# A planner's priorities get a table of offsets, and its durations are set anew

## The chip, the cores and the metric

One core of one Trainium2 chip runs the kernel as one program. The metric is the device time of one execution in microseconds. Every time of an engine below comes from one profiled execution.

## The reference, cut to what matters

```python
# attention-like part: x is (2, 3008, 256)
X = np.fft.fft(x, axis=1)            # over the 3008 positions
X = np.fft.fft(X, axis=2)            # over the 256 features
x = X.real                            # 6016 tokens x 256
# first MLP: w_in 256x2048, w_out 2048x256
h = x @ w_in
g = np.maximum(h, 0.0) ** 2
x = g @ w_out
# second MLP, same sizes: a rational function between the two products
h = x @ w_in2
P = a[0] + a[1] * h + a[2] * h**2 + a[3] * h**3
Q = 1.0 + abs(b[0]) * abs(h) + abs(b[1]) * h**2
out = (P / (Q + 1e-06)) @ w_out2
```

Everything is in float32. The kernel gets float32 accuracy from a rounded matmul type by splitting each operand into a high and a low part and adding three products (high-high, low-high, high-low).

## The kernel before, in words

**Tiles and stages.** The 6016 tokens are twelve tiles: tile 0 has 384 columns, tiles 1 to 11 have 512. The transform over the 3008 positions is split into 47 and 64 points. The 47-point part runs at the start for all tokens (`um`, `uo`); the 64-point part and the feature transform, called DFT below, run per tile in two or three jobs. One job is `fm` (two matmuls, L504 and L505), `fv` (ScalarE copy, L513), `fs` (matmuls, L526 and L528), `fe` (ScalarE, L536), `ff` (VectorE, L550 and L554); tiles 0 and 1 also have `fn` (ScalarE).

Layer 1 takes a tile in 16 chunks of 128 hidden features. A chunk is `h1` (TensorE: twelve matmuls for tiles 0 and 1, L674 and L676; seven for the others, L691 and L693), then, for tiles 2 and up, `b1` (ScalarE, L726), `s1` and `s2` (VectorE, L736), `r1` (ScalarE relu, L746), `a1` and `i1` (ScalarE squares, L752 and L756), `c1` (the low part, L761, on GpSimd; on VectorE for tiles 0 and 1), and `o1` (TensorE, six matmuls, L717), which adds the chunk into two PSUM banks `o1a` and `o1b` (tile 0 uses `o2a` and `o2b`). After the last chunk comes the hand-over to layer 2: `xh` (ScalarE, L767, two operations) and `xl` (VectorE, L772, two operations) turn the sums into the split input of layer 2. Only `xl` gives the two banks back.

Layer 2 takes tile 0 whole and each other tile in two halves of 256 columns. The halves are numbered 1 to 22, so that tile 1 has halves 1 and 2, and tile 11 has 21 and 22. A unit is two hidden chunks of one half: `h2` (TensorE, twelve matmuls, L661), `u` and `t1` (ScalarE, L779 and L784), `q`, `t2`, `t3` (VectorE, L790, L798, L802), `w`, `y`, `z` (ScalarE, L794, L807, L811), `gh`, `m`, `e` (VectorE, L824, L830, L837), `c2` (GpSimd, L841) and `o2` (TensorE, twelve matmuls, L717, into bank `o2a`). `t3` gives the bank of `h2` back. `oa` copies a finished half out. The units of the last two halves use other buffers, and GpSimd does their `gh` as well (L822).

At the start both layers' weights are converted on the chip from float64 bits: per chunk `wa` (ScalarE), `wc`, `w1`, `w2`, `w3` (VectorE), for layer 1 also `we`, then `wh` (ScalarE) and `wl` or `W` (VectorE). The raw weights of layer 2 lie in buffers of the tag `g2` until `w3` has read them, and `gh` of layer 2 takes buffers of the same tag.

**What sets the order.** Nothing is reordered on the chip: each engine runs its instructions in the order in which they were issued, and waits on semaphores for others. That order is made by a list scheduler, the class `Queues`, when the program is built. Every step is added with an engine, a cost in microseconds, a place, what it needs, and which buffers it takes and gives. `Queues.run` repeats one step: among all operations that are ready it takes the one with the smallest start that the costs allow, and among those with the same start the one with the smaller place:

```python
rank = (start, op["place"], op["n"])
if best is None or rank < best[0]:
    best = rank, op
```

A place is therefore a due time in chunks: tile t has its layer 1 at 16 t + chunk, its DFT from 16 (t - 1) + 1.05, its hand-over at 16 t + 15.5, its layer 2 from 16 (t + 1) + 1.04, and some constants (`LAG1`, `LAG2`, `LATE`) move `o1`, `o2` and the last tiles. The costs are the functions `act`, `dve`, `pool_tt`, `mm4` and `mm`: for an operation of n columns they give its time on ScalarE, VectorE, GpSimd, and TensorE with a float32 matmul or with the rounded type. A buffer tag has a fixed number of slots (`SLOTS`): two of `g1` for layer 1's split activations, three of `g2` for layer 2's, one each of the PSUM banks `o1a`, `o1b`, `o2a`, `o2b`, `p0` to `p3`. `h1`, `h2` and the DFT share `p0` to `p2`, and from tile 1 or 3 on `o2b` too. ScalarE and VectorE thus have work of the DFT, the weights, both layers and the hand-over in one queue each.

Of the kernel before, what the change touches and what calls it, by code (L numbers as in the profile page):

```python
# [58 lines left out]

def f32(ap):  # L60
    return ap.bitcast(F32)


class Queues:
# [6 lines left out]
    def add(self, key, engine, cost, place, fn, needs=(), take=(), give=(), lat=0.15, after=(),  # L71
            port=False):
        op = dict(n=len(self.ops), engine=engine, cost=cost, place=place, fn=fn, needs=needs, after=after,
                  take=take, give=give, lat=lat, port=port or engine == "POOL")
        self.ops.append(op)
        self.by_key[key] = op
# [61 lines left out]
def act(n, psum=False, ptr=0):  # L138
    return (n + (61 if psum else 112)) / 1200 + 0.093 * ptr
# [4 lines left out]


def pool_tt(n):
    return n * 2.52 / 1200 + 0.27


def mm4(n):  # L150
    return 4 * n / 2400 + 0.007


def mm(n):
    return max(n, 256) * 0.000448 + 0.003


@with_exitstack
def body(ctx: ExitStack, tc: tile.TileContext, x0, xf, w1i, w1o, w2i, w2o, a_in, b_in,
# [20 lines left out]
    a0, a1, a2, b0 = (ab[:, i:i + 1] for i in (0, 1, 2, 4))  # L180
# [20 lines left out]
    queues = Queues(SLOTS)  # L201
    add = queues.add
# [11 lines left out]
    for i, (o, a) in enumerate(((ab[:, 0:4], a_in.partition_broadcast(128)),  # L214
# [3 lines left out]
        needs=[("const", 3)])  # L218
# [31 lines left out]
    def u_mm(c, dc, tag):  # L250
        PU[c, dc] = p = ps(tag, [128, 4, 128])
        d = slice(dc * 128, (dc + 1) * 128)
        if c == 0:
            for i in range(4):
                nc.tensor.matmul(p[:, 0, 0:96], XT[c][0:96, i, d], c47_t[0:96, 3 + i], start=(i == 0), stop=(i == 3))
        else:
            for i in range(0, XN[c], 2):
                k, m = 3 * (i // 2), min(2, XN[c] - i)
                nc.tensor.matmul(p[:, i:i + m, 0:94], XT[c][:, k + 2, d], c47_t[:, 1:1 + m, 0:94], start=True, stop=False)
                for h in range(m):  # L260
                    nc.tensor.matmul(p[:, i + h, 0:94], XT[c][:, k + h, d], c47_t[:, 0, 0:94], start=False, stop=(h == m - 1))
# [35 lines left out]
    for c in range(NC):  # L297
        place = -32 + c
        n = XN[c]
        add(("x", c), "SP" if c else "ACT", 0.54 * n if c else 0.5, place if c else -50, lambda c=c: x_load(c), take=("xt",),  # L300
            lat=X_LAT if c > 1 else 4.0 if c else 5.0,
            after=[("wd", W_FIRST[c] - 1)] if W_FIRST[c] else [])

        if HOT[c - 1] and c:
            add(("hot", c), "PE", 0.222 * HOT[c - 1], place - 0.5, lambda c=c: hot(HOT[c - 1], "p0"), take=("p0",), give=("p0",),
                needs=[("um", c - 1, 1)])
        tags = tuple(U_TAGS[(2 * c + dc) % len(U_TAGS)] for dc in range(2))
        for dc in range(2):
            add(("um", c, dc), "PE", (0.39 * n + 0.06 * (n == 1)) if c else 0.9, place, lambda c=c, dc=dc, g=tags[dc]: u_mm(c, dc, g),
                needs=[("x", c)] + ([("hot", c)] if c and HOT[c - 1] and not dc else []), take=(tags[dc],), give=("xt",) if dc else (), lat=0.2)  # L310
        before = [("um", c, 1)]
        cuts = [("uo", 0, 94), ("ux", 94, 96)] if c == 0 else [("uo", 0, 94)]
        if c >= NC - U_SPLIT:
            cuts = [("uo", 0, U_CUT), ("ur", U_CUT, 92), ("uo2", 92, 94)]
            cuts = [cuts[0], cuts[2], cuts[1]]
        for i, (key, lo, hi) in enumerate(cuts):
            w = (hi - lo) * n
            at = U_REST if key == "ur" else place
            add((key, c, "c"), "ACT", act(w, True), at, lambda c=c, lo=lo, hi=hi: u_copy(c, lo, hi),
                needs=[("um", c, 0)] + ([(cuts[0][0], c, "c")] if i else []), take=() if i else ("g",),  # L320
                give=tags[:1] if i == len(cuts) - 1 else (), lat=0.2)
            for part in range(2):
                add((key, c, part), "DVE", dve(w), at,
                    lambda c=c, part=part, lo=lo, hi=hi: u_out(c, part, lo, hi), needs=before + [(key, c, "c")],
                    give=(tags[1], "g") if part and i == len(cuts) - 1 else (), lat=0.2)
                before = [(key, c, part)]
# [19 lines left out]
    def w_abs(j):  # L346
        CW[j] = sb("cw", (128, 512))
        nc.scalar.activation(out=CW[j], in_=RW[j][:, :, 1].bitcast(F32), func=ACTF.Abs)
# [83 lines left out]
    wl = [(m, i) for m in (1, 2) for i in range(NF)]  # L432
    for j, w in enumerate(wl):
        m, i = w
        place = W_AT[m - 1] + i
        raw, cmp = W_TAGS[m - 1][j % len(W_TAGS[m - 1])], "cw"
        after = []
        add(("wd", j), "SP", 1.5, place - 4, lambda j=j, w=w: w_load(j, *w), take=(raw,), lat=DMA_LAT,
            after=([("wd", j - 1)] if j else []) + [("x", c) for c in range(NC) if c < NC and W_FIRST[c] <= j])
        add(("wa", j), "ACT", act(512), place, lambda j=j: w_abs(j), needs=[("wd", j)], take=(cmp,),  # L440
            after=after + ([("wa", j - 1)] if j else []))
        add(("wc", j), "DVE", dve(512, True), place, lambda j=j: w_clamp(j), needs=[("wa", j)], port=True)
        add(("w1", j), "DVE", dve(512, True), place, lambda j=j: w_b1(j), needs=[("wc", j)], port=True)
        add(("w2", j), "DVE", dve(512), place, lambda j=j: w_b2(j), needs=[("w1", j)], port=True)
        add(("w3", j), "DVE", dve(512), place, lambda j=j: w_b3(j), needs=[("w2", j)], give=(raw,), port=True)
        done = ("w3", j)
        if m == 1:
            for part in range(2):
                add(("we", j, part), "DVE", dve(128), place, lambda j=j, p=part: w_eo(j, p), needs=[done],
                    take=() if part else ("eo",), port=True)  # L450
                done = ("we", j, part)
        parts = (256, 256) if m == 1 else (512,)
        for k, n in enumerate(parts):
            last = k == len(parts) - 1
            add(("wh", j, k), "ACT", act(n), place, lambda j=j, w=w, k=k: w_hi(j, *w, k),
                needs=[done] + (["released"] if m == 2 else []))
            add(("W",) + w if last else ("wl", j), "DVE", dve(n), place, lambda j=j, w=w, k=k: w_lo(j, *w, k),
                needs=[("wh", j, k)] + ([("wl", j)] if last and k else []),
                give=((cmp, "eo") if m == 1 else (cmp,)) if last else (), port=True)
# [140 lines left out]
    for t in range(T):  # L600
# [5 lines left out]
        for i, k in enumerate(jobs):  # L606
            if t == 0:
                place, gap = -12 + i, F_GAP0
# [302 lines left out]
    for t, (tile1, col, width) in enumerate(SUB):  # L911
# [47 lines left out]
        else:  # L959
            add(("oa", t), "ACT", act(width, True), place, lambda t=t: out_part(t, 0), needs=done, lat=2.5, take=("os",), give=("os",))  # L960
            add(("ob", t), "DVE", dve(width), place, lambda t=t: out_part(t, 1), needs=[("oa", t)], take=("os",),
                give=("os", "o2a", "o2b"), lat=2.5)

    for fn in queues.run():
        fn()

# [105 lines left out]
```

## Time and profile before

| | us |
|---|---|
| median of three runs | 1063.56 (1063.4 to 1064.38) |
| the profiled execution itself | 1065.41 |
| its span, first to last instruction | 1063.6 |
| TensorE busy (matmuls) | 1030.7, 97% |
| weight loads busy | 972.5, 91% |
| VectorE busy | 1003.8, 94% |
| ScalarE busy | 965.7, 91% |
| GpSimd busy | 487.8, 46% |
| mean granted TensorE clock | 0.995 |

The span leaves out what lies before the first and after the last instruction, 1.8 us here. The profile calls the engines PE (TensorE), PEld (its weight loads, which overlap its matmuls), DVE (VectorE), ACT (ScalarE), POOL (GpSimd) and SP (SyncE, which issues DMAs). An engine's busy time is the union of its instructions; an instruction's recorded duration contains the end of its write, so that the next can begin before it ends. In the views by stretch the engines stand in the order PE, PEld, DVE, ACT, POOL, each with its busy time and its number of instructions, then the granted clock, the DMA engines' busy share and GB/s. A granted clock of 1.00 is 2.4 GHz and 0.50 is 1.2 GHz. Numbers such as L717 are lines of the kernel before.

### The profile page before, as it was taken

The numbers are of one execution on the slowest core, as the hardware profiler recorded it, in microseconds if no ns is written. First come the engines' busy times: TensorE is split into PE (matmuls) and PEld (weight loads), VectorE is DVE, ScalarE is ACT, GpSimd is POOL, SyncE is SP. The second block draws the span as 40 slices with busy tenths as digits, with TensorE's granted clock in tenths as the row PEclk, the third lists the DMA queues.
The fourth block names the chain that finished last, engine by engine and source line by source line (L and its number), as shares of the span: only waits on it lengthen the run. The fifth ranks groups of instructions, "written<-read, shape, count | busy, mean of one in ns | idle before, by whom it ended". The sixth has DMA issues, their size and how long they took to land.

```text
span 1063.6 us, 20889 instructions
## 1 busy us (share of the span) xinstructions
PE 1030.7 (97%) x7538; PEld 972.5 (91%) x7538; DVE 1003.8 (94%) x1789; ACT 965.7 (91%) x1921; POOL 487.8 (46%) x373
## 2 busy tenths in 40 slices
PE   9999988999999999999999999999999999999986
PEld 9888977899999999989999999999999999999986
DVE  5999999989999999999999999999999999989998
ACT  3779998889999999899999999999999999999996
POOL 0000034445555555454555545545555545545576
PEclk9999999989999999999999999999999999999999
DMA  9664400000000000000000000000000000000000
GB/s 342 214 208 129 140 1 1 18 8 11 11 11 12 1 21 11 10 11 12 2 20 12 1 21 11 2 21 11 2 20 12 2 11 11 2 10 11 1 11 21
DMA packets 26941, 36.92 MB, mean 35 GB/s; under 512 B 2349, under 2 KB 19445, under 8 KB 26837
## 3 DMA queue, kind: packets, MB, share of 16 engines
q1 hardware_dynamic: 26725, 35.19, 9.9%
q8 instruction: 60, 0.98, 0.4%
q10 hardware_dynamic: 112, 0.39, 0.1%
q14 instruction: 44, 0.36, 0.1%
HBM read 26.74 MB, written 8.80 MB: 33 GB/s over the span
## 4 chain that ended last, share of the span: by engine, by line
PE 66%; DVE 16%; ACT 13%; issue 3%; DMA 1%; POOL 0%; POOLq 0%; SPq 0%; DVEq 0%; ACTq 0%
PE o2a L717 18%; PE p L661 12%; PE o1a L717 9%; PE o1b L717 9%; PE p L691 7%; PE o2b L661 5%; PE o2b L691 2%; DVE u L790 2%; DVE g L824 2%; ACT t L784 2%; DVE p L830 1%; ACT y L807 1%; DVE t L802 1%; DVE t L798 1%; PE p L693 1%
## 5 line engine op out<-in xcount | busy, mean ns | idle before, releaser
L841 POOL TENSOR_TENSOR g<-t,y 128x512 fp32r<-128x512 f32 (+1 forms) x182 | 247.8, 1362 | 378.3 <-DVE t L837 292.1
L761 POOL TENSOR_TENSOR g<-g,g 128x512 fp32r<-128x512 f32 x160 | 212.6, 1329 | 180.6 <-ACT g L756 131.8
L717 PE MATMUL o2a<-g,w2hi 128*128 128x256 f32 (+1 forms) x1440 | 259.7, 282 | 6.2 <-POOL g L841 6.0
L717 PEld LDWEIGHTS o2a<-g,w2hi 128*128 128x128 f32 x1440 | 209.1, 189 | 12.6 <-POOL g L841 8.9
L717 PE MATMUL o2a<-g,w2lo 128*128 128x256 f32 (+1 forms) x720 | 144.0, 280 | 0.0
L824 DVE SCALAR_TENSOR_TENSOR g<-t,ab,y 128x512 fp32r<-128x512 f32 (+1 forms) x176 | 137.8, 787 | 6.4 <-ACT y L811 4.6
L717 PE MATMUL o1a<-g,w1hi 128*128 128x512 f32 x352 | 139.5, 396 | 0.4 <-POOL g L761 0.4
L717 PE MATMUL o1b<-g,w1hi 128*128 128x512 f32 x352 | 138.4, 393 | 0.0
L830 DVE SCALAR_TENSOR_TENSOR p<-u,g 128x512 f32<-128x512 f32 (+1 forms) x176 | 136.4, 775 | 0.6
L837 DVE SCALAR_TENSOR_TENSOR t<-t,ab,p 128x512 f32<-128x512 f32 (+1 forms) x176 | 128.1, 728 | 0.5
L794 ACT ACTIVATE u<-u 128x512 f32<-128x512 f32 (+1 forms) x176 | 109.5, 622 | 14.3 <-DVE u L790 13.7
L661 PE MATMUL p<-x2h,w2hi 128*128 128x256 f32 (+1 forms) x540 | 110.7, 286 | 9.7 <-DVE t L802 5.8
L811 ACT ACTIVATE y<-y 128x512 f32<-128x512 f32 (+1 forms) x185 | 115.6, 625 | 1.4
L790 DVE SCALAR_TENSOR_TENSOR u<-u,ab,p 128x512 f32<-128x512 f32 (+1 forms) x135 | 98.0, 726 | 16.9 <-ACT t L784 16.2
L746 ACT ACTIVATE g<-g 128x512 f32<-128x512 f32 x160 | 101.3, 633 | 13.6 <-DVE g L736 12.4
L807 ACT ACTIVATE y<-u 128x512 f32<-128x512 f32 (+1 forms) x176 | 109.1, 621 | 4.2 <-DVE g L761 0.2
L752 ACT ACTIVATE g<-g 128x512 fp32r<-128x512 f32 (+1 forms) x174 | 109.1, 627 | 2.0 <-PE o1b L717 0.7
L717 PEld LDWEIGHTS o2a<-g,w2lo 128*128 128x128 f32 x720 | 110.3, 189 | 0.0
L756 ACT ACTIVATE g<-g 128x512 f32<-128x512 f32 (+1 forms) x174 | 108.9, 626 | 1.1
L661 PE MATMUL p<-x2h,w2lo 128*128 128x256 f32 (+1 forms) x540 | 108.0, 281 | 0.0
L661 PE MATMUL p<-x2l,w2hi 128*128 128x256 f32 (+1 forms) x540 | 107.7, 281 | 0.0
L736 DVE TENSOR_TENSOR g<-p,bc 128x256 f32<-128x256 f32 x250 | 101.1, 416 | 4.2 <-ACT bc L726 2.8
(271 smaller groups left out, 2776.0 us busy)
## 6 DMA issues: line engine op xcount, KB each, us to landing
g<-in_dram SPq DMA_DIRECT2D x48, 256.0 KB
xt<-in_dram SPq DMA_DIRECT2D x15, 384.0 KB
out_dram<-os SPq DMA_DIRECT2D x22, 256.0 KB
udram<-U SPq DMA_DIRECT2D x4, 640.0 KB
ut<-udram SPq DMA_DIRECT2D x10, 256.0 KB
x2h<-in_dram SPq DMA_DIRECT2D x8, 256.0 KB
x2l<-in_dram SPq DMA_DIRECT2D x8, 256.0 KB
x<-qdram SPq DMA_DIRECT2D x30, 1.0 KB
```

The source lines that it names most:

```text
L661: nc.tensor.matmul(h[:, c * n:(c + 1) * n], l[:, k, :], r[:, k], start=(q == 0), stop=(q == 5))
L717: nc.tensor.matmul(O[t][e], l[:, e * 128:(e + 1) * 128], r[:, c * n:(c + 1) * n], start=(i == 0 and q == 0 and (e == 0 or not one)), stop= ...
L752: nc.scalar.activation(out=e["gh"], in_=e["g"], func=ACTF.Square)
L761: eng.tensor_tensor(out=e["gl"], in0=e["g"], in1=f32(e["gh"]), op=ALU.subtract)
L790: nc.vector.scalar_tensor_tensor(out=e["w"], in0=w, scalar=b0, in1=H2[t, j], op0=ALU.add, op1=ALU.mult)
L794: nc.scalar.activation(out=w, in_=w, func=ACTF.Abs)
L807: nc.scalar.activation(out=e["z"], in_=e["w"], func=ACTF.Abs_reciprocal_sqrt, bias=Q1)
L811: nc.scalar.activation(out=z, in_=z, func=ACTF.Square)
L824: nc.vector.scalar_tensor_tensor(out=e["gh"], in0=e["t1"], scalar=a0, in1=e["z"], op0=ALU.add, op1=ALU.mult)
L830: nc.vector.scalar_tensor_tensor(out=e["m"], in0=e["w"], scalar=Q1, in1=f32(e["gh"]), op0=ALU.add, op1=ALU.mult)
L837: nc.vector.scalar_tensor_tensor(out=e["t1"], in0=e["t1"], scalar=a0, in1=e["m"], op0=ALU.add, op1=ALU.subtract)
L841: (nc.vector if (t, j) in FIN else nc.gpsimd).tensor_tensor(out=e["gl"], in0=e["t1"], in1=e["z"], op=ALU.mult)
```

## The change

Four kinds of edit, none of which adds or removes an instruction. First, the costs of GpSimd's and TensorE's operations, of the 47-point transform's matmuls and of the weights' first ScalarE operation are replaced. Second, a function `ranks` names the groups that an operation belongs to: its kind, its tile (or half tile in layer 2), its stage, or its four-chunk block of weights (blocks 0 to 3 are layer 1's, 4 to 7 layer 2's). Third, a table `SHIFT` gives groups an offset. Fourth, before the planner runs, every operation's place is moved by the sum of its groups' offsets, divided by eight. For example, `o1` of tile 2 is in the groups ("layer1", 2), ("o1", 2) and ("op", "o1"), and gets (-42 + 232 - 6) / 8 = +23.

```diff
@@ -59,6 +59,58 @@
 
 def f32(ap):
     return ap.bitcast(F32)
+
+
+LAYER1 = ("h1", "r1", "b1", "s1", "s2", "a1", "i1", "c1")
+LAYER2 = ("h2", "u", "v", "t1", "q", "t2", "t3", "w", "y", "z", "P", "gh", "m", "e", "c2", "oa", "ob", "o2")
+DFT = ("fm", "fv", "fs", "fe", "ff", "fd", "fn")
+WEIGHTS = ("wa", "wc", "w1", "w2", "w3", "we", "wh", "wl")
+
+
+def ranks(key):
+
+    c = key[0] if isinstance(key, tuple) else key
+    if c == "W":
+        return [("weights", (key[1] - 1) * 4 + key[2] // 4)]
+    if c in WEIGHTS:
+        return [("weights", key[1] // 4)]
+    out = []
+    for name, ops in (("layer1", LAYER1), ("layer2", LAYER2), ("dft", DFT), ("o1", ("o1",)), ("h2", ("h2",)),
+                      ("o2", ("o2",)), ("x2", ("xh", "xl"))):
+        if c in ops:
+            out.append((name, key[1]))
+    return out + [("op", c)] if out else []
+
+
+SHIFT = {
+    ("dft", 0): 31, ("dft", 1): 195, ("dft", 2): 61, ("dft", 3): 41, ("dft", 4): 19, ("dft", 5): -7,
+    ("dft", 6): -2, ("dft", 7): 9, ("dft", 8): -2, ("dft", 9): 37, ("dft", 10): -87, ("dft", 11): -29,
+    ("h2", 0): -11, ("h2", 1): -20, ("h2", 2): -9, ("h2", 3): -28, ("h2", 4): -16, ("h2", 5): -18,
+    ("h2", 6): 3, ("h2", 7): 5, ("h2", 8): -23, ("h2", 9): 7, ("h2", 11): -16, ("h2", 12): -15, ("h2", 13): 3,
+    ("h2", 14): -36, ("h2", 15): 5, ("h2", 16): -36, ("h2", 17): 10, ("h2", 19): -556, ("h2", 20): -10,
+    ("h2", 21): -8, ("h2", 22): -13, ("layer1", 0): 22, ("layer1", 1): 45, ("layer1", 2): -42,
+    ("layer1", 3): 4, ("layer1", 5): -26, ("layer1", 6): 12, ("layer1", 7): -66, ("layer1", 8): -46,
+    ("layer1", 10): -8, ("layer1", 11): -1, ("layer2", 0): -5, ("layer2", 1): 24, ("layer2", 2): 28,
+    ("layer2", 3): 25, ("layer2", 4): 14, ("layer2", 6): -19, ("layer2", 7): -11, ("layer2", 8): 11,
+    ("layer2", 9): 13, ("layer2", 10): 3, ("layer2", 11): -5, ("layer2", 12): -2, ("layer2", 13): -9,
+    ("layer2", 14): -4, ("layer2", 15): 5, ("layer2", 16): 28, ("layer2", 17): 2, ("layer2", 19): -8,
+    ("layer2", 20): 4, ("layer2", 21): -44, ("layer2", 22): -38, ("o1", 0): 4, ("o1", 1): -33, ("o1", 2): 232,
+    ("o1", 3): 1009, ("o1", 4): -411, ("o1", 5): 11, ("o1", 6): -6, ("o1", 7): 47, ("o1", 8): 7,
+    ("o1", 9): -172, ("o1", 10): 27, ("o1", 11): -33, ("o2", 0): 10, ("o2", 1): -340, ("o2", 2): -39,
+    ("o2", 3): 93, ("o2", 5): -498, ("o2", 6): 97, ("o2", 7): 12, ("o2", 8): -15, ("o2", 9): 26,
+    ("o2", 10): 729, ("o2", 11): -638, ("o2", 12): 20, ("o2", 13): -599, ("o2", 14): 17, ("o2", 15): -2,
+    ("o2", 16): 207, ("o2", 17): -6, ("o2", 18): 10, ("o2", 19): -132, ("o2", 20): -391, ("o2", 21): 181,
+    ("o2", 22): 161, ("op", "P"): 20, ("op", "a1"): 3, ("op", "b1"): -9, ("op", "c1"): -9, ("op", "c2"): -62,
+    ("op", "e"): -51, ("op", "ff"): -1, ("op", "fm"): 1, ("op", "fs"): 2, ("op", "fv"): -228,
+    ("op", "gh"): -5, ("op", "h2"): -1, ("op", "i1"): -97, ("op", "m"): -11, ("op", "o1"): -6,
+    ("op", "o2"): 1, ("op", "oa"): -8, ("op", "ob"): -160, ("op", "q"): -2, ("op", "r1"): -5, ("op", "s1"): 1,
+    ("op", "s2"): -4, ("op", "t1"): -6, ("op", "t2"): 4, ("op", "t3"): 3, ("op", "u"): -1, ("op", "w"): 1,
+    ("op", "xh"): 363, ("op", "xl"): 323, ("op", "y"): 7, ("op", "z"): -1, ("weights", 0): 4,
+    ("weights", 1): -81, ("weights", 2): 20, ("weights", 3): 15, ("weights", 4): 24, ("weights", 5): -33,
+    ("weights", 6): 315, ("weights", 7): -29, ("x2", 0): 139, ("x2", 1): -7, ("x2", 3): 3, ("x2", 4): -65,
+    ("x2", 5): -14, ("x2", 6): 4, ("x2", 7): -10, ("x2", 8): -76, ("x2", 9): -45, ("x2", 10): 119,
+    ("x2", 11): -60,
+}
 
 
 class Queues:
@@ -144,15 +196,15 @@
 
 
 def pool_tt(n):
-    return n * 2.52 / 1200 + 0.27
+    return n * 2.35 / 1200 + 0.255
 
 
 def mm4(n):
-    return 4 * n / 2400 + 0.007
+    return n * 0.00139 + 0.003
 
 
 def mm(n):
-    return max(n, 256) * 0.000448 + 0.003
+    return max(n, 256) * 0.000444 + 0.0018
 
 
 @with_exitstack
@@ -306,7 +358,7 @@
                 needs=[("um", c - 1, 1)])
         tags = tuple(U_TAGS[(2 * c + dc) % len(U_TAGS)] for dc in range(2))
         for dc in range(2):
-            add(("um", c, dc), "PE", (0.39 * n + 0.06 * (n == 1)) if c else 0.9, place, lambda c=c, dc=dc, g=tags[dc]: u_mm(c, dc, g),
+            add(("um", c, dc), "PE", (0.383 * n + 0.06 * (n == 1)) if c else 0.9, place, lambda c=c, dc=dc, g=tags[dc]: u_mm(c, dc, g),
                 needs=[("x", c)] + ([("hot", c)] if c and HOT[c - 1] and not dc else []), take=(tags[dc],), give=("xt",) if dc else (), lat=0.2)
         before = [("um", c, 1)]
         cuts = [("uo", 0, 94), ("ux", 94, 96)] if c == 0 else [("uo", 0, 94)]
@@ -437,7 +489,7 @@
         after = []
         add(("wd", j), "SP", 1.5, place - 4, lambda j=j, w=w: w_load(j, *w), take=(raw,), lat=DMA_LAT,
             after=([("wd", j - 1)] if j else []) + [("x", c) for c in range(NC) if c < NC and W_FIRST[c] <= j])
-        add(("wa", j), "ACT", act(512), place, lambda j=j: w_abs(j), needs=[("wd", j)], take=(cmp,),
+        add(("wa", j), "ACT", act(512) + 0.055, place, lambda j=j: w_abs(j), needs=[("wd", j)], take=(cmp,),
             after=after + ([("wa", j - 1)] if j else []))
         add(("wc", j), "DVE", dve(512, True), place, lambda j=j: w_clamp(j), needs=[("wa", j)], port=True)
         add(("w1", j), "DVE", dve(512, True), place, lambda j=j: w_b1(j), needs=[("wc", j)], port=True)
@@ -961,6 +1013,9 @@
             add(("ob", t), "DVE", dve(width), place, lambda t=t: out_part(t, 1), needs=[("oa", t)], take=("os",),
                 give=("os", "o2a", "o2b"), lat=2.5)
 
+    for key, op in queues.by_key.items():
+        op["place"] += sum(SHIFT.get(g, 0) for g in ranks(key)) / 8
+
     for fn in queues.run():
         fn()
 
```

## Rows read from the trace of the kernel before

**Rows 1.** Busy time by stage: stretch, length, each engine's busy us (instructions), clock, DMA.

```profile
0.00:30.00 30.00, 28.82 (x208) 28.43 (x209) 18.78 (x51) 11.38 (x23) 2.51 (x7) 1.00 0.95 341
30.00:60.00 30.00, 26.22 (x191) 24.15 (x191) 28.26 (x75) 22.76 (x60) 0.00 (x0) 0.95 0.58 187
60.00:130.00 70.00, 68.68 (x481) 65.22 (x481) 67.61 (x144) 61.99 (x127) 0.00 (x0) 1.00 0.51 166
130.00:230.00 100.00, 90.00 (x523) 80.75 (x522) 93.51 (x179) 87.26 (x184) 41.08 (x34) 0.97 0.02 8
230.00:1000.00 770.00, 765.61 (x5729) 724.87 (x5728) 737.04 (x1247) 728.17 (x1427) 401.07 (x301) 1.00 0.03 10
1000.00:1064.00 64.00, 51.34 (x415) 49.12 (x415) 58.58 (x98) 54.12 (x104) 43.11 (x33) 1.00 0.04 13
```

**Rows 2.** The same view of the two stretches at half clock, and the tail.

```profile
57.06:60.47 3.41, 3.41 (x19) 3.41 (x18) 2.87 (x9) 2.76 (x7) 0.00 (x0) 0.50 0.58 193
214.07:220.90 6.83, 6.07 (x28) 6.10 (x29) 5.75 (x12) 4.46 (x8) 2.59 (x2) 0.50 0.08 29
1010.00:1055.00 45.00, 37.07 (x297) 35.25 (x295) 44.40 (x74) 44.22 (x87) 36.52 (x29) 1.00 0.04 13
```

**Rows 3.** TensorE's waits up to 230: total us, times, longest us.

```profile
PE p L661 <- DVE t L802: 3.3, 5, 1.2
PE p L691 <- DVE t L802: 3.1, 3, 1.3
PE p L691 <- DVE g L736: 1.4, 1, 1.4
PE p L674 <- DVE x1l L550: 1.3, 1, 1.3
```

**Rows 4.** TensorE's waits from 1000 on.

```profile
PE o2a L717 <- POOL g L841: 5.1, 5, 1.6
```

**Rows 5.** The chain that ended last: start, us, twelve merged matmuls.

```profile
227.87 1.38 PE o2a L717 x12
```

**Rows 6.** GpSimd's L841: count, then ns minimum/median/maximum.

```profile
L841 POOL TENSOR_TENSOR g<-t,y x182: 1027/1324/1822, 139.8 to 1055.8; 128x512 fp32r<-128x512 f32 x166, 128x384 fp32r<-128x384 f32 x16
```

**Rows 7.** TensorE's timeline: one chunk's o1, an h1, and what follows.

```profile
590.10 0.39 PE L717 MATMUL o1a<-g,w1hi 128*128 128x512 f32 x1
...
591.47 0.28 PE L691 MATMUL p<-x1h,w1hi 128*128 128x256 f32 x1
...
592.28 0.38 PE L504 MATMUL o2b<-cd_t,ut 128*128 128x128 f32 x2
```

**Rows 8.** VectorE's groups by line: busy us, mean ns, idle before.

```profile
L824 DVE SCALAR_TENSOR_TENSOR g<-t,ab,y 128x512 fp32r<-128x512 f32 (+1 forms) x176 | 137.8, 787 | 6.4 <-ACT y L811 4.6 <-PE o2a L717 1.0 <-ACT g L746 0.5
L830 DVE SCALAR_TENSOR_TENSOR p<-u,g 128x512 f32<-128x512 f32 (+1 forms) x176 | 136.4, 775 | 0.6
L837 DVE SCALAR_TENSOR_TENSOR t<-t,ab,p 128x512 f32<-128x512 f32 (+1 forms) x176 | 128.1, 728 | 0.5
L802 DVE SCALAR_TENSOR_TENSOR t<-t,ab,p 128x512 f32<-128x512 f32 (+1 forms) x140 | 101.4, 724 | 0.6
L736 DVE TENSOR_TENSOR g<-p,bc 128x256 f32<-128x256 f32 x250 | 101.1, 416 | 4.2 <-ACT bc L726 2.8 <-POOL g L761 1.4
L790 DVE SCALAR_TENSOR_TENSOR u<-u,ab,p 128x512 f32<-128x512 f32 (+1 forms) x135 | 98.0, 726 | 16.9 <-ACT t L784 16.2 <-PE o2a L717 0.2
L798 DVE TENSOR_TENSOR t<-t,p 128x512 f32<-128x512 f32 (+1 forms) x140 | 92.9, 664 | 0.0
```

**Rows 9.** Timelines around the hand-over of tile 6 (TensorE, ScalarE, VectorE, TensorE).

```profile
595.25 0.39 PE L717 MATMUL o1b<-g,w1hi 128*128 128x512 f32 x1
...
595.94 0.58 ACT L767 ACTIVATE x2h<-o1a 128x512 fp32r<-128x512 f32 x1
...
597.50 0.68 DVE L772 TENSOR_TENSOR x2l<-o1b,x2h 128x512 fp32r<-128x512 f32 x1
...
599.85 0.39 PE L717 MATMUL o1a<-g,w1hi 128*128 128x512 f32 x1
```

## The prediction

> **What bounds the kernel now.** I read the page's engine table first, then the busy time by stage, then who ended TensorE's waits, and last the timeline of single steps. TensorE is busy for 1030.66 of 1064 us, and from 230 to 1000 us for 765.61 of 770: a wall with 4.39 us of holes [rows 1]. Its idle time is 33.3 us in all; the other 28.9 lie at the ends: 1.18 us before 30, 3.78 us from 30 to 60, 1.32 us from 60 to 130, 10.00 us from 130 to 230, and 12.66 us after 1000, of which 7.93 lie between 1010 and 1055 [rows 1, 2]. Twice the granted clock halves (0.50, that is 1.2 instead of 2.4 GHz): for 3.41 us from 57.06, with TensorE busy throughout, and for 6.83 us from 214.07, with 6.07 busy [rows 2]. Half the busy time is what it cost: 1.7 and 3.0 us. So an order of issue can win at most about 33 + 5 us, and only at the two ends; in the middle it can only lose.
>
> The cause differs by place. From 130 to 230 VectorE is the slow server (93.51 of 100 busy) and TensorE waits for it to free an accumulation bank: its three longest sums of waits up to 230, 7.8 us, end on VectorE's L802 or L736 [rows 3]. In the tail VectorE (44.40 of 45) is full and TensorE waits for GpSimd's g of L841, 5.1 us in 5 waits [rows 2, 4].
>
> **What the change can do.** It adds and removes no instruction. Durations and places are the planner's, and a place counts only between operations of one engine that could start at the same instant. So every effect is one of order, and I price it stage by stage. Places below are offsets divided by 8; a tile has 16.
>
> *Durations.* The plan's twelve 256-column matmuls fall from 1.41 to 1.39 us; the chain shows 1.38 [rows 5]. GpSimd's 512-column operation falls from 1.345 to 1.258, while the row of L841 has a median of 1.324 recorded [rows 6]. By itself this moves nothing on the chip but the order. If the plan leans on GpSimd too early in the tail, the price is at most 5 waits by the 0.087 us taken off, 0.4 us; below, nothing. I take 0.2.
>
> *Layer balance from 130 to 230.* Layer 1 of tile 2 moves 5.25 places forward (-42/8), layer 2 of tile 1's halves 3 and 3.5 back, so layer 1 gains 8 to 9 chunks on layer 2. One layer-1 chunk gives TensorE 592.28 - 590.10 = 2.18 us of work [rows 7] for two VectorE operations of 0.416, 0.83 us. One layer-2 unit gives it twice 1.38 = 2.76 us for six VectorE operations, .726 + .664 + .724 + .787 + .775 + .728 = 4.40 us [rows 5, 8]. (Recorded durations overlap at their ends; the ratio is what I use.) Eight chunks pulled forward are 17.4 us for TensorE and 6.6 of VectorE, which would have run 1.5 units worth 4.1 us: 13.3 us more work for TensorE in a stage that lacks 10.00 + 3.0 = 13.0. The displaced 6.6 us of VectorE go behind 230, where VectorE has 770 - 737.04 = 33 us free [rows 1]. That is the upper end. Against it stand layer 1's two g1 buffers, its one pair of o1 banks, and o1 of tile 2 itself, which goes 23 places back (232 - 42 - 6, over 8): it fills holes and does not lead. The second layer's weight chunks 8 to 11 go 39 places back, which frees VectorE now but keeps their raw data in g2 buffers that layer 2 needs. Lower end: a loss of one more clock fall, 3.0 us. I take 8.0 of the 13.0, since the amount moved covers the lack.
>
> *Start, 30 to 60.* Room is 3.78 + 1.7 = 5.5 us. First-layer weight chunks 4 to 7 come 10 places forward, which feeds TensorE sooner. But tile 1's DFT goes 24 places back, behind weight conversion on VectorE, and h1 of tile 0 from chunk 4 on is issued behind h1 of tile 1: its waits (L674 on L550, 1.3 us [rows 3]) can grow. Lower end: two weight conversions in front of it, each estimated at seven VectorE operations as long as L736's 0.416 us [rows 8], 2.9 us, so some 6 us lost. I take 0.
>
> *Depth first.* e moves 6.4 places forward, the second square of layer 1 (i1) 12, layer 2's GpSimd operation c2 8. That brings g sooner to TensorE and costs banks, since L802 (t3) waits meanwhile: one e, 0.728 us, against a wait it ends. In the middle TensorE's backlog hides both. In the tail it helps: room 7.93 us, layer 2 of the last two half tiles also comes 5.5 and 4.75 places forward, but VectorE is 44.40 of 45 busy there, so only work done before 1010 shortens it. Ends: 0 and 5.1 us (all waits for g); I take 2.5.
>
> *Middle.* o1 of tile 3 goes 126 places back, o1 of tile 4 comes 52 forward, o2 of half tile 10 goes 92 back, of 11 comes 80 forward. With a backlog on TensorE this changes which buffer comes free, not its sum. The hand-over between the layers, xh and xl, goes 31 to 63 places back in ScalarE's and VectorE's queues. Today the last o1 matmul of tile 6 starts at 595.25, xh at 595.94, xl ends at 597.50 + 0.68, and the next o1 starts at 599.85, with TensorE busy throughout [rows 9]. So 1.7 us of cover is left. Ends: all 4.39 us of holes closed, and the second rival's 16 us. I take a loss of 2.
>
> Sum: -8.0 + 0 - 2.5 + 2 + 0.2 = -8.3 us. Against the profiled execution, 1065.41 us with a span of 1063.6, that is 1057.1 and a span of 1055.3. The median is 1063.56, 1.85 below the profiled execution, so 1055.3 is forecast for it; I say 1055.
>
> *A rule against the row.* TensorE's busy share of 97% leaves 33 us. The Trainium skill (Perfetto Trace Analysis, Identifying the Most-Contended Engine) holds matmul busy time to be a poor measure of what is left and takes the busy share of weight loads instead. Taken as it stands, that gives 1064 less the six rows' sum of 972.54, 91 us, 45 of them in the middle, and a gain there would be open. The trace does not bear it out for this kernel: from 230 to 1000 weight loads are busy for 724.87 us while matmuls are for 765.61, so a full TensorE shows 0.947 of weight loads here, and 972.54/0.947 = 1027 leaves 37 us, near the 33 [rows 1].
>
> **Rivals.**
> *Slower by the hand-over.* xh and xl run only when ScalarE and VectorE have nothing else ready. Until then o1's only banks are held and layer 1 stands; TensorE lives on layer 2 alone and loses 4.40 - 2.76 = 1.64 us for each unit that VectorE takes first. One unit at each of 10 tiles is 16.4 us; with the gain above, 1055.3 + 16.4 = 1072. It decides from 0.83 us a tile. For it: VectorE is 95.7% busy in the middle [rows 1], so empty moments are rare. Against it: layer 1 then has no work to offer, so both queues run dry within a unit, and L790, which opens a unit, already waits 16.9 us in all [rows 8]; the 1.7 us of cover also hide one unit's loss.
> *No change.* VectorE's total, 1003.79 us over the six rows, is fixed; what is moved out of 130 to 230 makes it the bound later, or the start loses what the next stage gains. For it: 737.04 of 770 is close. Against it: 33 us free there against 6.6 moved. Time 1063.5.
> *More.* The stage from 130 to 230 is filled, its clock fall goes (13.0), half of the tail's 7.93 and of the start's 5.5 too: 19.7 less a loss of 1.5 in the middle, 1045. For it: the amount moved suffices. Against it: three stages must all come out well.
>
> **How the numbers follow.** Forecast 0.56 (own range 1049 to 1061), more 0.14, no change 0.09, slower by the hand-over 0.21. About 0.2%, 2 us, is what a measurement of this kernel can tell from no change; so faster 0.70, same 0.09, slower 0.21. The range 1043 to 1070 holds the forecast, nearly all of the larger gain and the smaller half of the slower case (up to half a unit a tile).
>
> **What would show it.** The windows: 130 to 230 with under 4 us idle and no half clock near 214 says the balance step is right; more than 10 says it is wrong. From there to 1000, over 8 us idle with waits of L661, L691 or L717 on the hand-over's L772 is the rival. From 30 to 60, more than 6 us idle makes the step on tile 1's DFT wrong. The tail is right if its waits for g fall below 3 us. The forecast as a whole is wrong if the time falls outside 1049 to 1061, and its mechanism is wrong if the time falls but the idle time from 130 to 230 does not.

## The result and the profile after

The changed kernel takes 1048.64 us in the median (1048.35 to 1050.88, four runs) against 1063.97 for the kernel before in the same series: a ratio of 0.986, with a 95% interval of 0.9843 to 0.9877. The profiled execution took 1048.59 us with a span of 1046.6, which is 17.0 us less span than before. Every line of the kernel before stands 52 lower in the changed one: L713 is the old L661, L743 the old L691, L769 the old L717, L788 the old L736, L824 the old L772, L854 the old L802, L889 the old L837 and L893 the old L841.

The busy time by stage of the changed kernel answers to [rows 1] (engines in the same order):

```profile
0.00:30.00 30.00, 28.64 (x211) 28.23 (x211) 18.63 (x51) 11.47 (x23) 2.51 (x7) 1.00 0.96 349
30.00:60.00 30.00, 25.18 (x185) 22.58 (x184) 28.47 (x77) 21.68 (x59) 0.00 (x0) 1.00 0.54 179
60.00:130.00 70.00, 69.85 (x490) 66.33 (x489) 67.09 (x142) 63.03 (x130) 0.00 (x0) 1.00 0.49 165
130.00:230.00 100.00, 96.54 (x603) 89.94 (x602) 98.16 (x191) 93.22 (x202) 45.81 (x37) 0.98 0.03 9
230.00:1000.00 770.00, 765.26 (x5771) 727.17 (x5769) 744.72 (x1265) 727.63 (x1435) 413.87 (x304) 1.00 0.03 10
1000.00:1047.00 47.00, 36.18 (x288) 34.17 (x288) 40.97 (x69) 38.56 (x76) 32.85 (x26) 0.99 0.05 18
```

From 130 to 230 TensorE's idle time fell from 10.00 to 3.46 us, and its instructions in these 100 us rose from 523 to 603. VectorE, the slow server there, went from 93.51 to 98.16 us busy. From 30 to 60 TensorE idles 4.82 us instead of 3.78. The two half-clock stretches of [rows 2] became one in this execution; in a second profiled execution of the same kernel, with the same order on every engine, there were two again:

```profile
45.63:49.04 3.41, 3.41 (x17) 3.41 (x18) 3.22 (x8) 2.98 (x9) 0.00 (x0) 0.50 0.65 227
144.61:148.02 3.41, 2.94 (x9) 2.94 (x10) 3.41 (x8) 2.50 (x7) 1.02 (x1) 0.50 0.00 0
```

In the first execution, the same view of its one stretch and of the stage from 230 to the end of the last `o1` matmul of tile 11 (980.58) and the tail behind it:

```profile
144.65:148.06 3.41, 3.41 (x12) 3.41 (x12) 3.41 (x9) 2.70 (x7) 1.03 (x1) 0.50 0.00 0
230.00:980.58 750.58, 749.45 (x5641) 712.11 (x5640) 725.50 (x1235) 709.99 (x1403) 403.68 (x297) 1.00 0.03 10
980.58:1043.00 62.42, 51.97 (x420) 49.23 (x419) 60.18 (x99) 55.62 (x107) 43.04 (x33) 1.00 0.03 10
```

The kernel before, cut at the same event (996.15):

```profile
230.00:996.15 766.15, 761.97 (x5701) 721.52 (x5700) 733.23 (x1241) 724.44 (x1421) 399.75 (x300) 1.00 0.03 10
996.15:1060.00 63.85, 54.96 (x445) 52.47 (x443) 62.39 (x104) 57.25 (x109) 44.44 (x34) 1.00 0.03 10
```

Middle: 4.18 us idle before, 1.13 after. Tail: 8.89 before, 10.45 after, in a tail that is 1.43 us shorter (63.85 to 62.42) and has 25 matmuls fewer: work moved out of it, but what is left waits more. TensorE's waits up to 230, in answer to [rows 3], and those behind 980.6, in answer to [rows 4]:

```profile
PE p L713 <- DVE t L854: 2.3, 2, 1.3
PE o2a L769 <- DVE g L813: 1.3, 2, 0.7
PE p L578 <- ACT v L565: 1.2, 1, 1.2
...
PE p L743 <- DVE g L788: 0.5, 1, 0.5
```

```profile
PE o2a L769 <- POOL g L893: 6.3, 8, 1.5
PE p L713 <- DVE x1h L887: 2.5, 2, 1.5
...
```

The wait for a bank (L713 on L854) fell from 3.3 to 2.3 us, the one of L743 on L854 (3.1 us before) is gone, and 6.3 us of the tail still go to GpSimd's g.

**Idle time hides a third of the holes.** Idle time went from 33.3 to 25.4 us over the stages, 8 us, but the span fell by 17. A matmul of 256 columns is recorded with some 0.28 us while the next one starts 0.115 us behind it [rows 5, 7], so the first 0.16 us of each hole count as busy, and matmuls at half clock count as busy throughout. I therefore took, from the trace, the time from each matmul's start to the next one's start, less the median of that time for its line and shape (7,537 intervals), and summed it by stage. This gives 50.1 us for the kernel before and 34.1 for the changed one; the difference of 16.0 covers the 17.0 of the span but for 1. It is the measure in the table below. The second profiled execution of the changed kernel gives some 35 us. How the matmuls are grouped for the median matters most where holes are small: by other groupings the middle comes to between 10.6 and 15.4 us before and between 5.0 and 7.4 after, but it always falls, by 5 to 8 us.

### The profile page after: what moved, and what is told of

It reads as the page before. It is cut to its first block, busy times and chain, and to the rows that moved or that the text cites. A ratio compares the mean times of both kernels' runs of the same rounds, so it can differ in the third digit from the quotient of the medians.

```text
span 1046.6 us, 20738 instructions
## 1 busy us (share of the span) xinstructions
PE 1021.6 (98%) x7538; PEld 968.4 (93%) x7538; DVE 998.0 (95%) x1789; ACT 955.6 (91%) x1921; POOL 495.0 (47%) x373
## 4 chain that ended last, share of the span: by engine, by line
PE 76%; DVE 9%; ACT 9%; DMA 3%; issue 2%; POOL 1%; POOLq 0%; SPq 0%; ACTq 0%; DVEq 0%
PE o2a L769 20%; PE p L713 15%; PE o1a L769 10%; PE o1b L769 10%; PE p L743 8%; PE o2b L713 5%; PE o2b L743 2%; PE p L745 1%; DMA g<-in_dram 1%; DVE g L876 1%; DMA xt<-in_dram 1%; PE o2b L769 1%; DVE p L882 1%; ACT t L836 1%; DVE t L854 1%
## 5 line engine op out<-in xcount | busy, mean ns | idle before, releaser
L893 POOL TENSOR_TENSOR g<-t,y 128x512 fp32r<-128x512 f32 (+1 forms) x182 | 250.5, 1376 | 248.7 <-DVE t L889 182.2
L813 POOL TENSOR_TENSOR g<-g,g 128x512 fp32r<-128x512 f32 x160 | 216.3, 1353 | 285.9 <-ACT g L808 237.0
L769 PE MATMUL o2a<-g,w2hi 128*128 128x256 f32 (+1 forms) x1440 | 258.7, 280 | 6.3 <-POOL g L893 6.3
L769 PEld LDWEIGHTS o2a<-g,w2hi 128*128 128x128 f32 x1440 | 209.2, 188 | 12.6 <-POOL g L893 7.9
L769 PE MATMUL o2a<-g,w2lo 128*128 128x256 f32 (+1 forms) x720 | 143.6, 279 | 0.0
L769 PE MATMUL o1a<-g,w1hi 128*128 128x512 f32 x352 | 139.5, 396 | 0.0
L769 PE MATMUL o1b<-g,w1hi 128*128 128x512 f32 x352 | 138.3, 393 | 0.0
L882 DVE SCALAR_TENSOR_TENSOR p<-u,g 128x512 f32<-128x512 f32 (+1 forms) x176 | 132.0, 750 | 0.1
L889 DVE SCALAR_TENSOR_TENSOR t<-t,ab,p 128x512 f32<-128x512 f32 (+1 forms) x176 | 127.5, 724 | 0.3
L863 ACT ACTIVATE y<-y 128x512 f32<-128x512 f32 (+1 forms) x185 | 117.8, 637 | 1.2
L713 PE MATMUL p<-x2h,w2hi 128*128 128x256 f32 (+1 forms) x540 | 109.7, 284 | 7.3 <-DVE x1h L887 2.5
L788 DVE TENSOR_TENSOR g<-p,bc 128x256 f32<-128x256 f32 x260 | 106.0, 414 | 9.7 <-POOL g L813 7.6
L798 ACT ACTIVATE g<-g 128x512 f32<-128x512 f32 x160 | 101.8, 637 | 13.7 <-DVE g L788 13.2
L769 PEld LDWEIGHTS o2a<-g,w2lo 128*128 128x128 f32 x720 | 109.8, 188 | 0.0
L713 PE MATMUL p<-x2h,w2lo 128*128 128x256 f32 (+1 forms) x540 | 108.3, 282 | 0.0
L713 PE MATMUL p<-x2l,w2hi 128*128 128x256 f32 (+1 forms) x540 | 108.1, 282 | 0.0
```

Of the source, the lines that this page charges most:

```text
L713: nc.tensor.matmul(h[:, c * n:(c + 1) * n], l[:, k, :], r[:, k], start=(q == 0), stop=(q == 5))
L769: nc.tensor.matmul(O[t][e], l[:, e * 128:(e + 1) * 128], r[:, c * n:(c + 1) * n], start=(i == 0 and q == 0 and (e == 0 or not one)), stop= ...
L813: eng.tensor_tensor(out=e["gl"], in0=e["g"], in1=f32(e["gh"]), op=ALU.subtract)
L863: nc.scalar.activation(out=z, in_=z, func=ACTF.Square)
L882: nc.vector.scalar_tensor_tensor(out=e["m"], in0=e["w"], scalar=Q1, in1=f32(e["gh"]), op0=ALU.add, op1=ALU.mult)
L889: nc.vector.scalar_tensor_tensor(out=e["t1"], in0=e["t1"], scalar=a0, in1=e["m"], op0=ALU.add, op1=ALU.subtract)
```

## The experiments

Two theories stood against each other. Theory A is the prediction's: each offset does its work in its stage, and the stages add up. By theory B, the list scheduler decides step by step, so one early difference changes all that follows; the table and the costs fit one particular course, and only as a whole. Beside them, theory C held that the corrected costs alone make the gain. Holes by stage as just defined, in us, with the span of each profiled execution; the last two columns are the planner's own end (the largest start plus cost after it has placed its last operation, which is its arithmetic and no measurement) and the span less that:

```
kernel                    0-130  130-230  230-950  950-end   all    span   planner  span-planner
before                      8.6     17.6     10.6     13.4   50.1  1063.6   1065.3     -1.7
changed                     7.4      7.1      5.0     14.6   34.1  1046.6   1036.1     10.5
e1  costs only              9.6     14.2     12.6     15.9   52.3  1065.8   1055.1     10.7
e2  table, old costs        7.5      8.9     26.1     20.7   63.1  1076.8   1077.9     -1.1
e3  table until 230         7.7      6.1     17.3     16.1   47.1  1060.5   1050.1     10.4
e4  table from 230          9.2     14.6     13.0     14.6   51.4  1063.7   1052.2     11.5
e5  hand-over back          7.7     17.4     18.2     19.1   62.3  1076.7   1063.3     13.4
e6  balance back            8.9     18.5     23.4     23.2   73.9  1087.6   1078.9      8.7
e7  divided by 9           11.0      9.5     38.0     23.8   82.2  1095.7   1085.3     10.4
e8  + 273 offsets           3.9      6.2      4.2     13.9   28.1  1041.6   1030.8     10.8
e9  old costs + 447         5.9      8.8     18.6     14.8   48.1  1061.6   1051.3     10.3
```

**Costs without the table.**

```diff
-    for key, op in queues.by_key.items():
-        op["place"] += sum(SHIFT.get(g, 0) for g in ranks(key)) / 8
```

> The new costs without the table of offsets. Theory A (effects are local to a stage, as in the prediction): costs alone only reorder near ties, 1060 to 1064 us, idle time of TensorE from 130 to 230 still 8 to 12 us. Theory B (table and costs are one fitted whole; the order is one particular outcome of the list scheduler): an order like any other, 1060 to 1068. Theory C (the corrected costs are what helps, since the old ones priced TensorE 2% too high): most of the gain is here, 1049 to 1054.

Measured 1066.97 us, ratio 1.0022 (1.001 to 1.0035). Theory C falls: corrected costs alone win nothing and lose a little.

**The table with the old costs.**

```diff
-    return n * 2.35 / 1200 + 0.255
+    return n * 2.52 / 1200 + 0.27
...
-    return max(n, 256) * 0.000444 + 0.0018
+    return max(n, 256) * 0.000448 + 0.003
...
```

> The table of offsets with the old costs. Theory A: the offsets move the same work forward whatever the costs, so most of the 15 us stays, 1049 to 1055 us, idle from 130 to 230 under 5 us. Theory B: the offsets fit only the course that the planner takes with the new costs; with others they are as good as random and cost new holes, 1068 to 1090, slower than before. Theory C: as before, 1060 to 1066.

Measured 1078.91 us, ratio 1.0142 (1.0124 to 1.0161). The offsets that won 15 us with one set of costs lose 15 with another, in which a rounded matmul costs 2% more, GpSimd's operation 7% and a float32 matmul of 128 columns 22%. Theory A falls here, and the time lies in theory B's range. The busy time by stage says how: the stage that was to gain still gains, and the middle pays.

```profile
130.00:230.00 100.00, 95.45 (x583) 87.79 (x582) 95.83 (x184) 92.22 (x200) 42.35 (x36) 0.98 0.02 8
230.00:980.00 750.00, 735.58 (x5455) 693.56 (x5453) 701.14 (x1196) 686.06 (x1356) 387.21 (x287) 1.00 0.03 10
```

From 130 to 230 TensorE idles 4.55 us, from 230 to 980 it idles 14.42.

**The offsets only up to 230, and only from 230.**

```diff
-                        rank = (start, op["place"], op["n"])
+                        rank = (start, op["place"] + (op["shift"] if start < 230 else 0), op["n"])
...
-        op["place"] += sum(SHIFT.get(g, 0) for g in ranks(key)) / 8
+        op["shift"] = sum(SHIFT.get(g, 0) for g in ranks(key)) / 8
```

(The second kernel has `start >= 230`.)

> New costs; the offsets count only for operations that the planner starts before 230 us, so that the order up to about there is that of the changed kernel, and the places after it are those of before. Theory A: the stage from 130 to 230 keeps its gain (idle under 4 us) and the rest runs as before: 1053 to 1057 us. Theory B: the same stage gain up to 230, but the order behind it is an unfitted one and gives part back in holes after 230: 1054 to 1066, idle from 230 to 1000 over 6 us.

> New costs; the offsets count only for operations that the planner starts from 230 us on. Theory A: the early stage is as with the new costs alone, and the middle and the tail keep what the change won there, some 5 us: 1056 to 1060 us. Theory B: the offsets meet another state at 230 than the one that they were fitted to and win nothing: 1060 to 1070, with holes after 230.

Measured 1062.22 us, ratio 0.9978 (0.9967 to 0.999), and 1066.68, ratio 1.0025 (1.0014 to 1.0035). The first is the sharpest test of the prediction's sum, since the stage from 130 to 230 has its whole gain:

```profile
130.00:230.00 100.00, 96.48 (x610) 89.50 (x610) 99.21 (x192) 93.93 (x204) 46.28 (x38) 1.00 0.03 9
230.00:980.00 750.00, 744.25 (x5534) 703.37 (x5533) 713.31 (x1211) 696.34 (x1378) 389.41 (x291) 1.00 0.03 10
```

TensorE idles 3.52 us there, as in the changed kernel, at a full clock. Yet 2 of 15 us remain, because the holes come back behind 230: 17.3 us from 230 to 950 where the changed kernel has 5.0. A gain in one stage is only lent until the order behind it can keep it. The second kernel loses 0.25% against before: the late offsets are worth nothing on another course. Both times lie in theory B's ranges and outside theory A's.

**The hand-over back at its old place.**

```diff
-        op["place"] += sum(SHIFT.get(g, 0) for g in ranks(key)) / 8
+        if key[0] not in ("xh", "xl"):
+            op["place"] += sum(SHIFT.get(g, 0) for g in ranks(key)) / 8
```

> The changed kernel with the hand-over xh and xl back at its old places; all other offsets and the costs stay. Theory A (local effects): pushing the hand-over back was a small cost, some 2 us as the prediction put it, so 1046 to 1049 us, like the changed kernel or better. Theory B (one fitted whole): a whole that misses a piece, 1055 to 1075, with holes in all stages.

Measured 1078.31 us, ratio 1.0126 (1.0104 to 1.0148). Theory A falls. The time is 3 us above theory B's range, and the holes are not in all stages: before 130 there are 7.7 us, as in the changed kernel (7.4), and 10 us more from 130 to 230, 13.2 in the middle and 4.5 at the end.

**The three offsets of the layer balance taken out.**

```diff
+    for g in (("layer1", 2), ("layer2", 1), ("layer2", 2)):
+        del SHIFT[g]
```

> The changed kernel without three offsets: layer 1 of tile 2 (-42), layer 2 of half tiles 1 and 2 (+24, +28). Theory A: the stage from 130 to 230 loses what the prediction put down to this balance, 8 to 10 us of idle time there, the rest stays: 1055 to 1058 us. Theory B: holes behind 230 too, more of them than in the stage: 1060 to 1090.

Measured 1089.01 us, ratio 1.0216 (1.0183 to 1.0248), in theory B's range. The stage does lose what the prediction put there (18.5 us of holes against 7.1), but the middle and the tail lose 27 more. So taking a group out does not measure what the group brings: it measures another course. I can't tell from it how much of the stage's gain the balance itself made.

**Every offset 11% smaller.**

```diff
-        op["place"] += sum(SHIFT.get(g, 0) for g in ranks(key)) / 8
+        op["place"] += sum(SHIFT.get(g, 0) for g in ranks(key)) / 9
```

> The same table divided by 9 instead of 8: every offset keeps its sign and its rank among the others and is 11% smaller. Theory A: what was moved forward is still moved forward, 1047 to 1053 us. Theory B: the ties that the offsets were fitted to fall the other way, and one early difference changes all that follows: 1060 to 1095, slower than before more likely than not.

Measured 1096.08 us, ratio 1.0284 (1.026 to 1.0308): the slowest of all, 1 us above theory B's range, with all signs and ranks as in the table.

```profile
130.00:230.00 100.00, 94.09 (x579) 86.17 (x578) 94.21 (x181) 92.43 (x199) 42.00 (x35) 1.00 0.03 10
230.00:980.00 750.00, 730.09 (x5376) 684.84 (x5375) 687.94 (x1180) 677.35 (x1336) 375.88 (x280) 0.99 0.03 10
```

19.91 us of idle time from 230 to 980, where the changed kernel has next to none. VectorE idles 62 us in the same stretch: neither is full. The largest of VectorE's waits there is for GpSimd's low part of layer 1 (230 to 980):

```profile
DVE g L788 <- POOL g L813: 31.9, 21, 3.7
```

**A finer table, and the same game with the old costs.** The first kernel adds offsets of single operations to the changed kernel, the second adds such offsets to the kernel before, with its old costs and no table. In both they were picked by letting the planner try offsets and keeping those with which it ends earlier by its own clock.

```diff
+FINE = {...}   # operation number: eighths of a place
...
+        op["place"] += FINE.get(op["n"], 0) / 8
```

> The changed kernel with further offsets for 273 single operations, picked so that the planner's own clock ends some 5 us earlier. Theory B (one fitted whole: an order that ends earlier by the planner's clock ends earlier on the chip): 1041 to 1046 us, TensorE's idle time after tile 11's last o1 matmul and before 230 smaller, no new holes in the middle. Rival (the fit is used up: further offsets fit only the planner's errors): 1047 to 1053.

> The kernel before, its old costs and places, with offsets for 447 single operations picked so that the planner's own clock ends some 14 us earlier. Theory B1 (the search for an order is what helps, with either costs): most of it arrives, 1049 to 1055 us. Theory B2 (only costs that follow the trace make such an order hold on the chip): less than half arrives, 1057 to 1066, with holes of TensorE in the middle that the planner does not see.

> The changed kernel once more, beside the two: 1047 to 1051 us.

Measured: 1043.63 us, ratio 0.9809 (0.9796 to 0.9822), for the finer table; 1063.76, ratio 0.9994 (0.9983 to 1.0005), for the old costs; 1049.38, ratio 0.9858 (0.9842 to 0.9873), for the changed kernel beside them. The first lies in theory B's range, the second in theory B2's. The finer table beats both kernels: 5.75 us below the changed one of the same series. With the old costs the planner believed in 14 us and the chip gave none that can be measured. Its stages, and those of the finer table:

```profile
130.00:230.00 100.00, 94.75 (x596) 86.52 (x595) 99.36 (x188) 92.47 (x197) 48.15 (x37) 1.00 0.03 8
230.00:980.00 750.00, 740.42 (x5519) 699.18 (x5519) 717.87 (x1207) 696.55 (x1378) 397.62 (x291) 1.00 0.03 10
```

```profile
130.00:230.00 100.00, 96.70 (x612) 90.68 (x611) 98.79 (x191) 93.59 (x201) 45.62 (x39) 0.98 0.02 8
230.00:980.00 750.00, 749.12 (x5623) 710.99 (x5622) 725.62 (x1231) 707.32 (x1400) 399.76 (x296) 1.00 0.03 10
```

With the old costs the early stage did gain (5.25 us idle against 10.00), and the middle lost it again (9.58 us idle). The last column of the table gives a reason. With the new costs the span is 8.7 to 13.4 us above the planner's end in all eight orders, so an order that ends earlier for the planner ends earlier on the chip, to within some 2.5 us either way. With the old costs the distance is -1.7, -1.1 and +10.3: there an earlier end for the planner says little. My reading, argued and shown only in part, is the 2% by which the old costs slow TensorE down (1.41 us for what takes 1.38 [rows 5]): an order picked against them counts on TensorE being late where on the chip it arrives and waits for VectorE. The planner's own arithmetic bears part of it out (each order held as it is, and only the durations exchanged; this is no run). With the old costs the searched order leaves TensorE no idle time from 230 to 950, with the new ones 10.2 us; on the chip 18.6 us of holes stand there. The rest stays open: by the new costs that order still ends 10.7 us before the order of the kernel before (1046.0 against 1056.7), and the chip gave 2.0 of span.

A rival is not excluded either. A search over 447 single operations may fit other errors of the planner, whatever the costs; against it, the 273 of the finer table held on the chip. The same search with the new costs but without the table was not measured, and the five costs that changed were not tried one by one.

## Why the prediction came out as it did

The forecast was 1055 (range 1043 to 1070) with faster at 0.70; 1048.64 lies inside the range, just below the forecast's own 1049 to 1061, and nearer to the larger rival's 1045 than to 1055. By the sign that the prediction set for itself, a time outside 1049 to 1061, the forecast as a whole was missed by 0.4 us; measured again, the kernel took 1049.38. The direction and the main stage were right; of the gain of 15 us some 9 were foreseen.

**Layer balance, 130 to 230: right in size, wrong in how.** Forecast 8.0 of 13.0 us. Measured by the prediction's own terms: 10.00 to 3.46 us idle and 3.0 to 1.7 us lost at half clock (half of the 3.41 us busy at 0.50), 7.8 us. So the sign for this step, under 4 us idle and no half clock near 214, came true. By the start-to-start measure it is 10.5 (17.6 to 7.1). But its working does not hold. Two readings of the table were off: `ranks` does not count `o1` to the group layer1, so `o1` of tile 2 goes (232 - 6) / 8 = 28.25 places back and not 23, and `h2` of half tile 1, which opens that half's units, moves 0.4 places and not 3. And the prediction pulled eight layer-1 chunks forward at the price of 1.5 layer-2 units. `s1` and `s2` of layer 1 in this stage, before and after:

```profile
130.00:230.00 100.00, 10.58 (x26) 0.97 0.02 8
```

```profile
130.00:230.00 100.00, 13.19 (x32) 0.98 0.03 9
```

`e` of layer 2, before and after:

```profile
130.00:230.00 100.00, 13.44 (x21) 0.97 0.02 8
```

```profile
130.00:230.00 100.00, 13.55 (x22) 0.98 0.03 9
```

Three chunks more (26 to 32 operations, two a chunk), and one unit more rather than 1.5 less. Nothing was displaced. The room came from VectorE's own idle time, 6.49 us before and 1.84 after, which the prediction read as a full engine because 93.51 of 100 looked full. VectorE's own waits between 20 and 230 name what it waited for, layer 2's t1 on ScalarE (before, then after; total us, times, longest us):

```profile
DVE u L790 <- ACT t L784: 4.6, 6, 1.7
```

```profile
DVE u L842 <- ACT t L836: 0.2, 1, 0.2
```

So the stage lacked ready work on both engines, and the new order had it.

**Start: right.** Forecast 0. From 30 to 60 the idle time grew by 1.04 us and the half-clock loss of 1.7 went (it is back in the second profiled execution, so this is no effect of the order alone); the holes by the other measure hardly moved, 8.6 to 7.4 up to 130.

**Tail: wrong.** Forecast a gain of 2.5 us. From the end of tile 11's `o1` to 1060 and 1043 TensorE's idle time rose from 8.89 to 10.45, and the waits for GpSimd's g from 5.1 to 6.3. The sign was that these waits fall below 3 us. VectorE stays 60.18 of 62.42 us busy. The step said itself that only work done before 1010 shortens the tail; it priced the offsets of the last halves all the same.

**Middle: wrong, and the largest miss.** Forecast a loss of 2 us, measured a gain of 3.05 in idle time and of some 5.6 by the other measure (10.6 to 5.0). The prediction called the middle a wall in which an order can only lose. By the busy time it was (99.4%); by the start-to-start measure it held 10.6 us of holes, most of them under what a recorded matmul covers.

**The slower rival's mechanism happened; from tile 2 on it cost nothing, at tile 1 TensorE waited.** The hand-over did go later, as the offsets say. At tile 8, where it took longest (TensorE, ScalarE, VectorE, TensorE):

```profile
734.72 0.39 PE L769 MATMUL o1b<-g,w1hi 128*128 128x512 f32 x1
...
738.20 0.61 ACT L819 ACTIVATE x2h<-o1a 128x512 fp32r<-128x512 f32 x1
...
743.76 0.68 DVE L824 TENSOR_TENSOR x2l<-o1b,x2h 128x512 fp32r<-128x512 f32 x1
...
746.40 0.40 PE L769 MATMUL o1a<-g,w1hi 128*128 128x512 f32 x1
```

From the start of the last `o1` matmul to the next `o1` it takes 11.68 us, where tile 6 of the kernel before took 4.60 [rows 9]. The rival priced this at 1.64 us a unit. TensorE had no wait in that stretch, since h1 of tile 9, which needs neither the o1 banks nor the hand-over, was there to run. The same holds for all tiles from 2 to 10: TensorE idles for 0.00 us in each of these stretches and its holes are at most 0.2 us, though they last 8.1 us in the mean instead of 5.0. At tile 1 it did not hold:

```profile
140.34 0.39 PE L769 MATMUL o1b<-g,w1hi 128*128 128x512 f32 x1
...
151.05 0.40 PE L769 MATMUL o1a<-g,w1hi 128*128 128x512 f32 x1
```

That stretch grew from 4.57 to 10.70 us. For its first 8.8 us TensorE ran nothing but layer 2, as the rival says, and waited 2.34 us for VectorE to free a bank (the two waits on L854 in the last section); before it idled 0.13 us. The second profiled execution has the same two waits (1.30 and 1.08 us). They are two thirds of the 3.46 us that it still idles from 130 to 230. The experiment that put the hand-over back lost 30 us against the changed kernel, but as with the balance that is another course and no price of the hand-over.

**The large offsets: nothing to price.** The prediction weighed `o1` of tile 3 at 126 places back and others at 50 to 90. Cut off at 24 places either way, the table gives the very same order, so that beyond this a number only says first or last; that kernel would be the same program.

**The sum: the step that failed as a method.** That -8.3 us came so near the fall in idle time, 8.0 us, is luck: the forecast was some 4 us too hopeful for the tail and some 5 us too gloomy for the middle, and the two nearly cancel. The rest of the 17 us lay in holes that busy time covers, which the sum did not look for. Stage terms were added as if each stage kept what it won. The kernel with the offsets up to 230 alone has the stage's gain and ends at 1062.22. And the chance for slower was reasoned from one mechanism, while the experiments show another: in the seven orders tried in which table or costs were not as in the change (the first seven of the experiments), the middle has 12.6 to 38.0 us of holes, where the changed kernel has 5.0.

The Trainium skill's rule that was weighed (Perfetto Trace Analysis, Identifying the Most-Contended Engine) calls matmul busy time a poor measure, and the middle bears that out: 99.4% busy, and 10.6 us of holes. The reason that the page gives is that pipelined instructions look smaller in the trace; here a record is longer than the spacing, 0.28 us against 0.115 [rows 5, 7]. Of the two measures that the page takes instead, the busy share of weight loads follows the change but not the level: they are busy for 972.54 us before and 968.43 after, for the same 7,538 loads, so that, as an estimate by that page, 91.5 and 78.6 us of room would be left, where the holes are 50.1 and 34.1.

## What to carry to other kernels

Where a planner makes the order, first make its costs agree with the trace, then search, and judge the two together: costs alone made it 0.2% slower, a search on the old costs gave nothing, both together 1.4% and a finer search 1.9%. (That the costs decided rests on one table and one searched order with the old costs.) Don't read a table of priorities entry by entry, and don't test it by taking entries out; in this scheduler an 11% change of all offsets cost 4.5% against the table as it was. To see how much a matmul-bound stretch still holds, sum start-to-start times over their median, not idle time.

## What was not expected of the hardware

The chip followed the new costs very closely. Between orders that differ by 54 us in span, the distance to the planner's end stayed within 8.7 to 13.4 us, although the costs are straight lines in the number of columns and know nothing of the clock's halves or of GpSimd's spread (L841 between 1.027 and 1.822 us [rows 6]). The narrow band alone does not single out the new costs: held in their order and priced at the old ones, the same eight kernels lie 3.2 to 8.9 us below the planner's end. Less expected was where the clock fell: in the changed kernel's execution it halved once while TensorE had work, at 144.65, right behind two waits for a bank of 1.26 and 1.08 us, and in the second execution at 144.61 in the same place (TensorE's timeline, idle time before in brackets), while the tail idles 3.48 of 10 us at a full clock (timeline of TensorE with idle time in brackets, then a stretch of the tail):

```profile
141.99 0.62 PE L713 MATMUL p<-x2h,w2hi 128*128 128x384 f32 x2 [1.26 <-DVE t L854]
...
144.38 0.80 PE L713 MATMUL p<-x2h,w2hi 128*128 128x384 f32 x2 [1.08 <-DVE t L854]
```

```profile
1030.00:1040.00 10.00, 6.52 (x48) 5.92 (x48) 9.57 (x19) 7.97 (x19) 8.99 (x8) 1.00 0.00 1
```
